# 64-point DFTs as three float32r products with operands split on ScalarE, VectorE and GpSimd, and steps placed by due date

## The chip, the cores and the metric

The kernel runs on one core of a Trainium2 chip. A core has five engines with a queue each, which run beside one another and wait for one another through semaphores: TensorE (PE; its weight loads are shown apart as PEld), VectorE (DVE), ScalarE (ACT), GpSimd (POOL) and SyncE (SP), which here only issues DMAs. The metric is the device time of one execution in microseconds (us), as the median of several runs.

## The reference

Two parts follow one another. The first is a circular convolution by FFT over the sequence: `X = rfft(x)` over 3008 positions for 8 batches and 256 channels, a product with a complex filter, and `irfft`. The second sends each of the 24064 tokens through a block with a rational activation:

```python
X = np.fft.rfft(x, axis=1);  Y = X * (filt_r + 1j * filt_i);  y = np.fft.irfft(Y, n=3008, axis=1)
h = y @ w_in                                    # 256 -> 2048
g = (a0 + a1*h + a2*h**2 + a3*h**3) / (1 + |b0|*|h| + |b1|*h**2 + 1e-6)
out = g @ w_out                                 # 2048 -> 256
```

Everything is float32, and the kernel must reach float32 accuracy.

## The kernel before

**Two number formats on TensorE.** A matmul whose operands are plain float32 is one instruction in the program and two records in the trace (x2). A float32r operand is one that was rounded when it was written; a matmul of float32r operands is one record. To keep the accuracy with float32r, an operand is split into `hi` (the rounded value) and `lo` (the rest, rounded), and a product is made of three matmuls: high weights by hi, high weights by lo, low weights by hi. The large products of the second part (h_u, lines 460 to 463, and o, lines 537 to 539) are made so. The convolution is in plain float32.

**The units.** The second part is cut into 47 token tiles of 512 and 16 slices of the hidden width: 752 units. A unit has six matmuls into a PSUM bank (h_u), a chain of ScalarE, GpSimd and VectorE operations that makes hi_u and lo_u, and six matmuls into o. The loop `pipeline` runs one step per unit, and step i issues on each engine what belongs to several units at once. The table ORDER gives the lags. On VectorE, in this order: hi_u of unit i-2 (line 514), then a convolution step if there is one, then `rest` of unit i-3 (line 522), `p` of unit i-1 (line 505), lo_u of unit i-3 (line 528). On GpSimd: the convolution step, then the product q_u by hi_u of unit i-2 (line 519), then line 500 for unit i-1. So `rest` of a unit waits for GpSimd's line 519, which was issued one step earlier. TensorE issues in step i: h_u of unit i, the convolution step, o of unit i-5 (i-6 for the first of a tile).

**The convolution.** Per batch the 3008 points are split as 47 by 64. Stage 1 has 16 matmuls s (line 300, 96 partitions); ScalarE copies each out of PSUM (s1e, line 263), and SP stores pairs of them in the DRAM scratch scr1 (line 304). Stage 2 loads it back (xin, line 339) and has, for 12 column blocks, the forward 64-point DFT y (line 348), VectorE's two products with the filter (lines 355 and 356), GpSimd's crosswise terms zw (four instructions, line 367) and their sum (line 372), and then the inverse 64-point DFT z (line 381), copied out of PSUM by ScalarE and VectorE in turn (lines 263 and 265) and stored in scr2. Stage 3 loads tl from scr2 and makes x (line 426), which ScalarE and VectorE split into the token operands xh and xl.

Batch one goes through all this before the loop. Batches two to eight (numbers 1 to 7 in the code) are spread over the steps of the loop by a generator `conv_items`, which yields before each s, y and z. The loop holds a credit that grows by RATES per step and pays COST for each such step; a batch may start EARLY units ahead. Stage 3 pieces come at steps 1 and 9 of a tile. GAP yields stand between stage 1 and stage 2. All engines but SP run in the order in which the program was written.

**Buffers.** Six PSUM banks are shared by the units and the convolution steps (class Banks: the bank free for longest is taken). zw has two buffers, `ev` two, xin four, filters f1 and f2 three each; z is made in place in f1.

## Time and profile before

| | |
|---|---|
| median of 3 runs | 2523.23 us (2522.63 to 2524.99) |
| the profiled execution | 2527.08 us |
| its span | 2525.1 us |
| busy share of the span | PE 98%, PEld 76%, DVE 90%, ACT 87%, POOL 74% |
| granted TensorE clock | 0.99 of full speed over the span |

The profile comes from one execution. A busy engine may be one whose instructions overlap: matmul records are modelled at their ends, so the pace of TensorE is read from starts. "Idle before" is time in which an engine stood still ahead of an instruction, and the releaser is what ended it. The timeline gives start, length, engine, line and operation of single instructions.

### The profile page before, as it was taken

Reading aid. Unit: us, or ns where it says so; the run is one execution under the profiler, and the core shown is the slowest. Engines: PE = TensorE matmul, PEld = TensorE weight load, DVE = VectorE, ACT = ScalarE, POOL = GpSimd, SP = SyncE. Lnnn points to the kernel's source line nnn. Section 1 sums busy time; section 2 is a strip of 40 time slices with the busy share of each in tenths; the row PEclk is TensorE's granted clock in tenths of the full one; section 3 lists DMA queues with packets and bytes.
Section 4 is the critical chain, followed back from the end, with each engine's and each line's share of the span. In section 5 each row is a group of like instructions: output and inputs, shape, how many; then the busy total and the mean of one; then the engine's idle time right before and its main releaser. Section 6 shows DMA issues by size and latency. Waiting matters only on the chain.

```text
span 2525.1 us, 35502 instructions
## 1 busy us (share of the span) xinstructions
PE 2464.8 (98%) x10456; PEld 1918.1 (76%) x10456; DVE 2264.6 (90%) x3573; ACT 2201.0 (87%) x4193; POOL 1856.3 (74%) x1984
## 2 busy tenths in 40 slices
PE   4799999999999999999999999999999999999998
PEld 1477777777777777878777777777777778888887
DVE  5789988999889998999889998899988999999998
ACT  4588889888988889888898889988898889999997
POOL 3468876887668876788668886688757887677776
PEclk8999999999999999999999999999999999999999
DMA  8643342222323222231322322222222211000000
GB/s 256 199 132 104 92 124 86 83 85 68 100 90 94 78 82 72 96 96 59 107 88 70 92 78 91 87 85 86 80 82 94 75 43 32 28 24 22 24 9 19
DMA packets 104364, 208.94 MB, mean 83 GB/s; under 512 B 9696, under 2 KB 59104, under 8 KB 104160
## 3 DMA queue, kind: packets, MB, share of 16 engines
q1 hardware_dynamic: 100944, 199.30, 25.8%
q10 hardware_dynamic: 3216, 7.27, 0.9%
q8 instruction: 85, 1.39, 0.2%
q14 instruction: 119, 0.97, 0.1%
HBM read 131.56 MB, written 74.97 MB: 82 GB/s over the span
## 4 chain that ended last, share of the span: by engine, by line
PE 89%; DVE 4%; POOL 2%; DMA 2%; issue 1%; ACT 1%; SPq 0%; ACTq 0%; DVEq 0%; POOLq 0%
PE o L538 13%; PE o L537 13%; PE o L539 13%; PE h_u L461 13%; PE h_u L460 13%; PE h_u L463 13%; PE x L426 4%; PE s L300 4%; PE y L348 3%; PE z L381 3%; DVE h_u L522 1%; POOL q_u L519 1%; POOL zw L367 1%; DMA scr<-s1e 1%; DVE h_u L505 1%
## 5 line engine op out<-in xcount | busy, mean ns | idle before, releaser
L519 POOL TENSOR_TENSOR q_u<-q_u,hi_u 128x512 f32<-128x512 f32 x752 | 975.1, 1297 | 470.6 <-DVE hi_u L514 451.8
L537 PE MATMUL o<-hi_u,wo_sb 128*128 128x512 f32 x1504 | 704.5, 468 | 0.0
L468 ACT ACTIVATE q_u<-h_u 128x512 f32<-128x512 f32 x752 | 450.3, 599 | 209.4 <-PE h_u L463 143.0
L522 DVE SCALAR_TENSOR_TENSOR h_u<-h_u,words_sb,q_u 128x512 f32<-128x512 f32 x752 | 564.0, 750 | 61.0 <-POOL q_u L519 59.6
L514 DVE SCALAR_TENSOR_TENSOR hi_u<-h_u,words_sb,a_u 128x512 fp32r<-128x512 f32 x752 | 557.4, 741 | 66.0 <-ACT a_u L490 64.1
L460 PE MATMUL h_u<-xh,wi_sb 128*128 128x512 f32 x1504 | 593.4, 395 | 1.8 <-DVE xl L438 1.2
L538 PE MATMUL o<-lo_u,wo_sb 128*128 128x512 f32 x1504 | 590.3, 393 | 2.8 <-DVE lo_u L528 2.8
L539 PE MATMUL o<-hi_u,wo_sb 128*128 128x512 f32 x1504 | 587.8, 391 | 0.0
L461 PE MATMUL h_u<-xl,wi_sb 128*128 128x512 f32 x1504 | 586.9, 390 | 0.2
L500 POOL TENSOR_SCALAR q_u<-q_u,words_sb 128x512 f32<-128x512 f32 x752 | 584.0, 777 | 1.3 <-ACT a_u L485 1.3
L505 DVE SCALAR_TENSOR_TENSOR h_u<-w_u,words_sb,h_u 128x512 f32<-128x512 f32 x752 | 559.9, 745 | 3.4 <-ACT w_u L475 3.4
L528 DVE TENSOR_TENSOR lo_u<-h_u,a_u 128x512 fp32r<-128x512 f32 x752 | 512.1, 681 | 0.1
L485 ACT ACTIVATE a_u<-q_u 128x512 f32<-128x512 f32 x752 | 475.6, 632 | 0.0
L490 ACT ACTIVATE a_u<-a_u 128x512 f32<-128x512 f32 x752 | 470.9, 626 | 0.0
L481 ACT ACTIVATE q_u<-q_u 128x512 f32<-128x512 f32 x752 | 469.3, 624 | 0.0
L463 PE MATMUL h_u<-xh,wi_sb 128*128 128x512 f32 x1504 | 463.9, 390 | 0.0
L475 ACT ACTIVATE w_u<-h_u 128x512 f32<-128x512 f32 x752 | 444.1, 590 | 0.3 <-POOL wi_sb L246 0.3
L538 PEld LDWEIGHTS o<-lo_u,wo_sb 128*128 128x128 f32 x1504 | 282.7, 188 | 113.1 <-issue 61.3
L537 PEld LDWEIGHTS o<-hi_u,wo_sb 128*128 128x128 f32 x1504 | 282.5, 188 | 112.8 <-issue 64.7
L460 PEld LDWEIGHTS h_u<-xh,wi_sb 128*128 128x128 f32 x1504 | 282.5, 188 | 70.1 <-DVE lo_u L528 5.8
L461 PEld LDWEIGHTS h_u<-xl,wi_sb 128*128 128x128 f32 x1504 | 282.6, 188 | 63.6 <-issue 3.1
L539 PEld LDWEIGHTS o<-hi_u,wo_sb 128*128 128x128 f32 x1504 | 282.4, 188 | 61.7
(95 smaller groups left out, 1874.4 us busy)
## 6 DMA issues: line engine op xcount, KB each, us to landing
xin<-xp SPq DMA_DIRECT2D x64, 384.0 KB, 3.8
scr<-s1e SPq DMA_DIRECT2D x64, 384.0 KB, 4.0
xin<-scr SPq DMA_DIRECT2D x48, 512.0 KB, 4.7
scr<-ev SPq DMA_DIRECT2D x96, 256.0 KB, 3.8
tl<-scr SPq DMA_DIRECT2D x64, 384.0 KB, 3.1
outT<-oe SPq DMA_DIRECT2D x47, 512.0 KB, 2.8
f<-fr SPq DMA_DIRECT2D x87, 256.0 KB, 4.1
f<-fi SPq DMA_DIRECT2D x87, 256.0 KB, 3.8
```

The costliest lines, as they stand in the source:

```text
L460: nc.tensor.matmul(o, w_in_part(0, f, cc), xh[:, cc, ts], start=cc == 0, stop=False)
L461: nc.tensor.matmul(o, w_in_part(0, f, cc), xl[:, cc, ts], start=False, stop=False)
L463: nc.tensor.matmul(o, w_in_part(1, f, cc), xh[:, cc, ts], start=False, stop=cc == 1)
L500: nc.gpsimd.tensor_scalar(out=self.q, in0=self.q, scalar1=AIK, scalar2=SGN, op0=ALU.mult, op1=ALU.add)
L505: v.scalar_tensor_tensor(out=H, in0=w, scalar=PK, in1=H, op0=ALU.add, op1=ALU.mult)
L514: nc.vector.scalar_tensor_tensor(out=self.hi, in0=self.H, scalar=self.p0, in1=self.a, op0=ALU.add, op1=ALU.mult)
L519: nc.gpsimd.tensor_tensor(out=self.q, in0=self.q, in1=self.hi.bitcast(F32), op=ALU.mult)
L522: nc.vector.scalar_tensor_tensor(out=self.H, in0=self.H, scalar=self.p0, in1=self.q, op0=ALU.add, op1=ALU.subtract)
L528: nc.vector.tensor_tensor(out=self.lo, in0=self.H, in1=self.a, op=ALU.mult)
L537: nc.tensor.matmul(o, w_out_part(0, f, dd), self.hi, start=f == 0, stop=False)
L538: nc.tensor.matmul(o, w_out_part(0, f, dd), self.lo, start=False, stop=False)
L539: nc.tensor.matmul(o, w_out_part(1, f, dd), self.hi, start=False, stop=f == 15)
```

## The change

The 64-point DFTs are made as three float32r matmuls in place of one float32 matmul: y in batches three to eight (72 of them), z in batches two to eight (84). The matrices are split once, at the end of the first batch (four small instructions). For y, the operand is split where stage 1 leaves PSUM: ScalarE writes hi (in place of its copy), and VectorE, at the end of the step, writes lo = PSUM - hi; scr1 then holds both halves, twice the bytes, with one store for each s and one load for each y. For z, ScalarE copies z to hi right after the inverse product before it, and GpSimd subtracts for lo, one step later, ahead of its other work of that step. The two halves lie in one buffer (tag raw). zw has one buffer in place of two.

The credit is gone. Each batch has a first step (`begin`) and a last one (`end`, three steps before its first stage 3 piece is wanted), and a convolution step is issued once the loop has reached its due place between them, in proportion to LOAD; TURN steps are kept free between stages 1 and 2.

```diff
+LOAD = dict(s=0.62, y=1.2, z=0.86), dict(s=0.76, y=1.03, z=0.86)
+REST = 3
...
+GAP = 1
+TURN = 4
...
-    scr1 = [dram.tile([K2, 128, C], F32, tag="scr1", name=f"scr1_{b}") for b in range(B)]
+    scr1 = [
+        dram.tile([K2, 128, 2, C], F32, tag="scr1", name=f"scr1_{b}") if b > 1
+        else dram.tile([K2, 128, C], F32, tag="scr1_0", name=f"scr1_{b}", bufs=2) for b in range(B)
+    ]
...
-            yield COST[0]
+            yield "s"
             k, pt = banks.tile(f"s1_{b}_{q}_{j}")
             nc.tensor.matmul(pt[:R1], a1_sb, xin[:, j], start=True, stop=True)
             yield
+            if b > 1:
+                split_rows(b, q, j, k, pt[:R1])
+                continue
             evac(EV1, ev[:, j], pt[:R1], 2 * q + j)
             banks.done(k, 0.5)
+        if b > 1:
+            return
...
+
+    def finish():
+        while pending:
+            pending.pop(0)()
+
+    def split_rows(b, q, j, bank, pt):
+
+        ev = conv.tile([R1, 2, 2, C], F32R, tag="ev", name=f"s1e{b}_{q}_{j}")
+        hi, lo = ev[:, :, 0], ev[:, :, 1]
+        pt = pt.rearrange("p (m c) -> p m c", c=C)
+        nc.scalar.activation(hi, pt, AF.Copy)
+
+        def lower():
+            v.tensor_tensor(out=lo, in0=pt, in1=hi.bitcast(F32), op=ALU.subtract)
+            banks.done(bank, 0.5)
+            m = 4 * q + 2 * j
+            dst = scr1[b].rearrange("k (g m) h c -> (k g) m (h c)", m=NH)[:, m : m + 2]
+            nc.sync.dma_start(dst.rearrange("r m c -> r (m c)"), ev.bitcast(F32).rearrange("p m h c -> p (m h c)"))
+
+        pending.append(lower)
+
...
+    def run_own(*key):
+        while own := [t for t in tasks if t[2] == key]:
+            tasks.remove(own[0])
+            own[0][3]()
...
+        def load_split(self, i):
+            if i < 12:
+                self.tin[i] = conv.tile([128, 2, 2, C], F32R, tag="xin", name=f"xin{self.b}_{i}", bufs=XB)
+                nc.sync.dma_start(
+                    self.tin[i].bitcast(F32), scr1[self.b][2 * i : 2 * i + 2].rearrange("k p h c -> p k h c")
+                )
+
+        def fetch(self, q):
+            (self.load_split if self.b > 1 else self.load)(q)
+
...
@@ -343,9 +398,16 @@
 
         def product(self, i):
             b, (q, j) = self.b, divmod(i, 2)
-            yield COST[1]
+            yield "y"
             bank, yt = banks.tile(f"y_{b}_{i}")
-            nc.tensor.matmul(yt, mats_sb[:, 0, :], self.flat(self.tin[q], j), start=True, stop=True)
+            if b > 1:
+                tin = self.tin.pop(i)
+                hi, lo = tin[:, :, 0], tin[:, :, 1]
+                nc.tensor.matmul(yt, fwd_sb[:, 0], hi, start=True, stop=False)
+                nc.tensor.matmul(yt, fwd_sb[:, 0], lo, start=False, stop=False)
+                nc.tensor.matmul(yt, fwd_sb[:, 1], hi, start=False, stop=True)
+            else:
+                nc.tensor.matmul(yt, mats_sb[:, 0, :], self.flat(self.tin[q], j), start=True, stop=True)
             yield
             self.z[i] = z, z2 = [self.flat(f_, j) for f_ in self.f[q]]
...
                 return
 
...
                 if WAITS[n]:
                     yield
             nc.gpsimd.tensor_tensor(out=z, in0=z, in1=zw, op=ALU.add)
+            if i == 0:
+                tasks.append((banks.now + 1, "post", (b, 0), lambda: self.split(0)))
+
+        def split(self, i):
+
+            if i == 12:
+                return
+            z = self.z[i][0]
+            part = conv.tile([128, 2, TT], F32R, tag="raw", name=f"zs{self.b}_{i}", bufs=1)
+            self.parts[i] = hi, lo = part[:, 0], part[:, 1]
+            nc.scalar.activation(hi, z, AF.Copy)
+
+            def lower():
+                nc.gpsimd.tensor_tensor(out=lo, in0=z, in1=hi.bitcast(F32), op=ALU.subtract)
+
+            tasks.append((banks.now + 1, "post", (self.b, i), lower))
 
         def inverse(self, i):
             b, (q, j) = self.b, divmod(i, 2)
             if j == 0:
                 self.ev[q] = self.tl("ev", q)
-            yield COST[2]
+            yield "z"
             bank, zt = banks.tile(f"z_{b}_{i}")
             z, z2 = self.z.pop(i)
-            nc.tensor.matmul(zt, mats_sb[:, 1, :], z, start=True, stop=b > 0)
-            if b == 0:
+            if b:
+                run_own(b, i)
+                hi, lo = self.parts.pop(i)
+                nc.tensor.matmul(zt, inv_sb[:, 0], hi, start=True, stop=False)
+                nc.tensor.matmul(zt, inv_sb[:, 0], lo, start=False, stop=False)
+                nc.tensor.matmul(zt, inv_sb[:, 1], hi, start=False, stop=True)
+            else:
+                nc.tensor.matmul(zt, mats_sb[:, 1, :], z, start=True, stop=False)
                 nc.tensor.matmul(zt, mats_sb[:, 2, :], z2, start=False, stop=True)
             yield
             evac(EV2 if b else "A", self.flat(self.ev[q], j), zt, i)
             banks.done(bank, 0.5)
+            if b:
+                self.split(i + 1)
...
         for i in range(13):
             if i < 12:
                 yield from s.product(i)
             if i > 0:
                 yield from s.inverse(i - 1)
+            if b > 1:
+                s.fetch(i + 2)
             if i % 2 == 0 and i // 2 + 2 < 6:
                 s.load_filter(i // 2 + 2)
-                s.load(i // 2 + 2)
...
         for _ in range(GAP):
             yield
+        finish()
         yield from stage2(b)
...
+        nc.scalar.activation(fwd_sb[:, 0], mats_sb[:, 0], AF.Copy)
+        nc.vector.tensor_tensor(out=fwd_sb[:, 1], in0=mats_sb[:, 0], in1=fwd_sb[:, 0].bitcast(F32), op=ALU.subtract)
+        nc.scalar.activation(inv_sb[:, 0], mats_sb[:, 1], AF.Copy)
+        nc.vector.tensor_tensor(out=inv_sb[:, 1], in0=mats_sb[:, 1], in1=inv_sb[:, 0].bitcast(F32), op=ALU.subtract)
...
+    latest = [g0 * G // T * 16 - 8 + XF for g0, _ in chunks]
+    for k in range(len(chunks) - 2, -1, -1):
+        latest[k] = min(latest[k], latest[k + 1] - 8)
+
+    def end(b):
+
+        return latest[8 * b] - REST
+
+    def begin(b):
+        return FIRST if b == 1 else end(b - 1)
+
+    def due(b, used, kind):
+        w = LOAD[b > 1]
+        total = 16 * w["s"] + 12 * (w["y"] + w["z"])
+        return begin(b) + (end(b) - begin(b) - TURN) * used / total + TURN * (kind != "s")
...
-            credit = min(credit + RATES[nxt > 1], 2.5)
...
-                if g1 * G <= t * T + RX and ((g0 if f > XF else g1) * G < T * (t + 2) or need < nxt):
+                if g1 * G <= t * T + RX and (i >= latest[xk] or need < nxt):
...
-            elif credit > 0 and i < n and not active and i >= last + PGAP and not (xgen and i > xi):
-                if gen is None and nxt < B and i >= FIRST and i >= 94 * nxt - 94 - EARLY:
-                    gen = conv_items(nxt)
-                    cost = next(gen)
-                if gen:
+            elif i < n and not active and i >= last + PGAP and not (xgen and i > xi):
+                if gen is None and nxt < B and i >= begin(nxt):
+                    gen, used = conv_items(nxt), 0
+                    kind = next(gen)
+                if gen and i >= due(nxt, used, kind):
                     next(gen)
-                    credit -= cost
+                    used += LOAD[nxt > 1][kind]
                     post.append("c")
...
             for name, lag in ORDER[:CPOS]:
                 step(lag, name)
+            run_tasks(i, "post")
...
+            run_tasks(i, "end")
+            finish()
```

**TensorE around y.** Batch five (number 4), block 4, step 295 before and step 316 after; h_u295 is the bank of unit 295, fwd_sb the split matrix, xin4_4 the loaded halves.

```order
L463 MATMUL h_u295_10782<-xh_613,wi_sb_76 128x512 x2
L348 MATMUL y_4_4_10789<-xin4_2_10311,mats_sb_78 128x512
L537 MATMUL o18_0_10751<-hi_u290_10690,wo_sb_77 128x512
L538 MATMUL o18_0_10751<-lo_u290_10738,wo_sb_77 128x512
L539 MATMUL o18_0_10751<-hi_u290_10690,wo_sb_77 128x512
```

After the change the same place reads:

```order
L552 MATMUL h_u316_11799<-xh_619,wi_sb_76 128x512 x2
L406 MATMUL y_4_4_11806<-xin4_4_11611,fwd_sb_79 128x512
L407 MATMUL y_4_4_11806<-xin4_4_11611,fwd_sb_79 128x512
L408 MATMUL y_4_4_11806<-xin4_4_11611,fwd_sb_79 128x512
L626 MATMUL o19_0_11587<-hi_u311_11715,wo_sb_77 128x512
L627 MATMUL o19_0_11587<-lo_u311_11765,wo_sb_77 128x512
L628 MATMUL o19_0_11587<-hi_u311_11715,wo_sb_77 128x512
```

One float32 matmul has become three float32r matmuls between the same neighbours; o follows five units behind h_u in both.

**GpSimd from one zw to the next.** The same batch, from the sum that belongs to block 4 to the zw of block 5; zs4_4 is the buffer of the split halves of block 4.

```order
L372 TENSOR_TENSOR f14_2_10305<-f14_2_10305,zw4_4_10806 128x512
L519 TENSOR_TENSOR q_u294_10769<-q_u294_10769,hi_u294_10833 128x512
L500 TENSOR_SCALAR q_u295_10801<-q_u295_10801,words_sb_81 128x512
L519 TENSOR_TENSOR q_u295_10801<-q_u295_10801,hi_u295_10865 128x512
L500 TENSOR_SCALAR q_u296_10837<-q_u296_10837,words_sb_81 128x512
L519 TENSOR_TENSOR q_u296_10837<-q_u296_10837,hi_u296_10905 128x512
L500 TENSOR_SCALAR q_u297_10869<-q_u297_10869,words_sb_81 128x512
L519 TENSOR_TENSOR q_u297_10869<-q_u297_10869,hi_u297_10934 128x512
L500 TENSOR_SCALAR q_u298_10909<-q_u298_10909,words_sb_81 128x512
L367 TENSOR_SCALAR zw4_5_10974<-f24_2_10306,sgn_sb_75 64x256 x4
L519 TENSOR_TENSOR q_u298_10909<-q_u298_10909,hi_u298_10965 128x512
```

After the change, from the same sum on:

```order
L434 TENSOR_TENSOR f14_2_11246<-f14_2_11246,zw4_4_11825 128x512
L608 TENSOR_TENSOR q_u315_11786<-q_u315_11786,hi_u315_11852 128x512
L589 TENSOR_SCALAR q_u316_11820<-q_u316_11820,words_sb_83 128x512
L608 TENSOR_TENSOR q_u316_11820<-q_u316_11820,hi_u316_11882 128x512
L589 TENSOR_SCALAR q_u317_11856<-q_u317_11856,words_sb_83 128x512
L608 TENSOR_TENSOR q_u317_11856<-q_u317_11856,hi_u317_11915 128x512
L589 TENSOR_SCALAR q_u318_11886<-q_u318_11886,words_sb_83 128x512
L448 TENSOR_TENSOR zs4_4_11923<-f14_2_11246,zs4_4_11923 128x512
L608 TENSOR_TENSOR q_u318_11886<-q_u318_11886,hi_u318_11957 128x512
L589 TENSOR_SCALAR q_u319_11919<-q_u319_11919,words_sb_83 128x512
L429 TENSOR_SCALAR zw4_5_12002<-f24_2_11247,sgn_sb_75 64x256 x4
L608 TENSOR_TENSOR q_u319_11919<-q_u319_11919,hi_u319_11993 128x512
```

The subtraction (line 448) stands between line 500 and line 519 of one step, so line 519 of that step comes behind it. zw of block 5 comes five steps after that of block 4 in both.

**VectorE at the end of a step with s.** Batch five, stage 1; s1e4 is the buffer of the split rows. Before, no VectorE instruction belongs to s, and a step there reads (units 251 to 253):

```order
L514 SCALAR_TENSOR_TENSOR hi_u252_9388<-h_u252_9307,words_sb_81,a_u252_9325 128x512
L522 SCALAR_TENSOR_TENSOR h_u251_9278<-h_u251_9278,words_sb_81,q_u251_9295 128x512
L505 SCALAR_TENSOR_TENSOR h_u253_9339<-w_u253_9359,words_sb_81,h_u253_9339 128x512
L528 TENSOR_TENSOR lo_u251_9400<-h_u251_9278,a_u251_9294 128x512
L514 SCALAR_TENSOR_TENSOR hi_u253_9419<-h_u253_9339,words_sb_81,a_u253_9357 128x512
```

After the change, in step 265, which holds the second s of the batch:

```order
L611 SCALAR_TENSOR_TENSOR h_u262_9902<-h_u262_9902,words_sb_83,q_u262_9933 128x512
L594 SCALAR_TENSOR_TENSOR h_u264_9978<-w_u264_9996,words_sb_83,h_u264_9978 128x512
L617 TENSOR_TENSOR lo_u262_10040<-h_u262_9902,a_u262_9932 128x512
L332 TENSOR_TENSOR s1e4_0_1_10031<-s1_4_0_1_10016,s1e4_0_1_10031 96x2x256
L603 SCALAR_TENSOR_TENSOR hi_u264_10063<-h_u264_9978,words_sb_83,a_u264_9994 128x512
```

The subtraction out of PSUM (line 332) stands behind lo_u and ahead of hi_u of the next step.

## Rows read from the trace of the kernel before

**Rows 1.** The page: the span, and busy time, share and instructions of each engine.

```profile
span 2525.1 us, 35502 instructions
...
PE 2464.8 (98%) x10456; PEld 1918.1 (76%) x10456; DVE 2264.6 (90%) x3573; ACT 2201.0 (87%) x4193; POOL 1856.3 (74%) x1984
```

**Rows 2.** Stretches in which the convolution is in stage 2 (206 to 324: batch two; the others: batches four, five and six): length, then busy us (and instructions) of PE, PEld, DVE, ACT and POOL, granted clock, DMA share, GB/s.

```profile
206.00:324.00 118.00, 117.50 (x493) 90.08 (x492) 109.82 (x172) 98.41 (x188) 102.58 (x120) 1.00 0.29 90
740.00:880.00 140.00, 140.00 (x598) 110.10 (x597) 132.00 (x209) 121.69 (x235) 119.25 (x136) 1.00 0.29 85
1030.00:1202.00 172.00, 171.88 (x745) 135.92 (x744) 162.10 (x255) 149.29 (x287) 142.70 (x161) 1.00 0.24 74
1320.00:1495.00 175.00, 174.62 (x755) 137.76 (x754) 162.93 (x256) 153.07 (x294) 141.94 (x161) 1.00 0.27 82
```

**Rows 3.** The timeline of TensorE in batch five, stage 2, from one y to the next: start us, length us. The rows of line 460 are the first matmul of a unit.

```profile
1082.79 0.39 PE L460 MATMUL h_u<-xh,wi_sb 128*128 128x512 f32 x1
...
1084.15 1.02 PE L348 MATMUL y<-xin,mats_sb 128*128 128x512 f32 x2
...
1086.40 0.39 PE L460 MATMUL h_u<-xh,wi_sb 128*128 128x512 f32 x1
...
1089.14 0.39 PE L460 MATMUL h_u<-xh,wi_sb 128*128 128x512 f32 x1
...
1090.50 1.02 PE L381 MATMUL z<-f,mats_sb 128*128 128x512 f32 x2
...
1091.59 0.40 PE L538 MATMUL o<-lo_u,wo_sb 128*128 128x512 f32 x1
...
1092.75 0.39 PE L460 MATMUL h_u<-xh,wi_sb 128*128 128x512 f32 x1
...
1095.48 0.39 PE L460 MATMUL h_u<-xh,wi_sb 128*128 128x512 f32 x1
...
1099.57 1.02 PE L348 MATMUL y<-xin,mats_sb 128*128 128x512 f32 x2
```

**Rows 4.** What VectorE waited for in the last three stretches of rows 2, in their order, the row of GpSimd's product from each: us in total, times, longest.

```profile
DVE h_u L522 <- POOL q_u L519: 7.9, 16, 1.0
...
DVE h_u L522 <- POOL q_u L519: 7.4, 17, 0.6
...
DVE h_u L522 <- POOL q_u L519: 7.5, 15, 0.8
```

**Rows 5.** The timeline of VectorE over the same y to y; in brackets, idle time before an instruction and what ended it.

```profile
1085.33 0.68 DVE L355 TENSOR_TENSOR f<-y,f 128x512 f32<-128x512 f32 x1
...
1087.84 0.68 DVE L528 TENSOR_TENSOR lo_u<-h_u,a_u 128x512 fp32r<-128x512 f32 x1
...
1089.55 0.76 DVE L522 SCALAR_TENSOR_TENSOR h_u<-h_u,words_sb,q_u 128x512 f32<-128x512 f32 x1 [0.37 <-POOL q_u L519]
...
1092.13 0.68 DVE L265 COPY ev<-z 128x512 f32<-128x512 f32 x1
...
1095.38 0.75 DVE L522 SCALAR_TENSOR_TENSOR h_u<-h_u,words_sb,q_u 128x512 f32<-128x512 f32 x1
...
1097.95 0.75 DVE L522 SCALAR_TENSOR_TENSOR h_u<-h_u,words_sb,q_u 128x512 f32<-128x512 f32 x1
...
1100.62 0.69 DVE L355 TENSOR_TENSOR f<-y,f 128x512 f32<-128x512 f32 x1
```

**Rows 6.** The timeline of GpSimd over the same stretch.

```profile
1086.17 1.96 POOL L367 TENSOR_SCALAR zw<-f,sgn_sb 64x256 f32<-64x256 f32 x4 [0.57 <-POOL q_u L500]
...
1094.88 0.78 POOL L500 TENSOR_SCALAR q_u<-q_u,words_sb 128x512 f32<-128x512 f32 x1
1095.75 1.30 POOL L519 TENSOR_TENSOR q_u<-q_u,hi_u 128x512 f32<-128x512 f32 x1
...
1098.19 1.30 POOL L519 TENSOR_TENSOR q_u<-q_u,hi_u 128x512 f32<-128x512 f32 x1 [0.37 <-DVE hi_u L514]
```

**Rows 7.** Groups by line over the whole span: count, then busy us, mean ns of one, idle us before them and what ended it.

```profile
L372 POOL TENSOR_TENSOR f<-f,zw 128x512 f32<-128x512 f32 x84 | 109.0, 1297 | 0.0
L348 PE MATMUL y<-xin,mats_sb 128*128 128x512 f32 x192 | 99.6, 602 | 19.5 <-issue 19.1 <-DVE ev L265 0.3
L381 PE MATMUL z<-f,mats_sb 128*128 128x512 f32 x180 | 92.4, 595 | 3.3 <-ACT fxl L329 3.3
L263 ACT ACTIVATE s1e<-s 96x512 f32<-96x512 f32 x128 | 75.1, 595 | 38.6 <-PE s L300 17.7 <-DMA scr<-s1e 12.4 <-DVE words_sb L187 7.8
...
L356 DVE TENSOR_TENSOR f<-y,f 128x512 f32<-128x512 f32 x90 | 61.1, 679 | 0.0
```

**Rows 8.** Two more stretches, columns as in rows 2: stage 1 of batch four falls into the first; in the second the loop has no stage 1 or 2 left to do.

```profile
614.00:722.00 108.00, 108.00 (x457) 82.88 (x457) 91.22 (x143) 97.98 (x189) 70.07 (x69) 1.00 0.27 83
2125.00:2400.00 275.00, 275.00 (x1252) 229.68 (x1251) 260.38 (x412) 263.90 (x509) 198.00 (x193) 1.00 0.07 22
```

**Rows 9.** The last stage 1 step of batch eight: SP's issues of the last store of scr1 and of the first load of it (timeline of SP).

```profile
1912.11 0.30 SPq L304 DMA_DIRECT2D scr<-s1e  x1
1915.14 0.38 SPq L339 DMA_DIRECT2D xin<-scr  x1
```

**Rows 10.** The page: DMA queue 1 (packets, MB, share of 16 engines), and loads of scr1 (count, KB each, median us from issue to landing).

```profile
q1 hardware_dynamic: 100944, 199.30, 25.8%
...
xin<-scr SPq DMA_DIRECT2D x48, 512.0 KB, 4.7
```

More of the change, by code (lines that the diff above doesn't have):

```diff
@@ L306, in stage1, with run_tasks @@
         )
+    pending = []
+    def finish():
[13 more added lines that the diff above has]
+        pending.append(lower)
+    tasks = []
+    def run_tasks(i, place):
+        ready = [t for t in tasks if t[0] < i or t[0] == i and t[1] == place]
+        for t in ready:
+            tasks.remove(t)
+            t[3]()
+    def run_own(*key):
+        while own := [t for t in tasks if t[2] == key]:
+            tasks.remove(own[0])
+            own[0][3]()
     class Stage2:
         def __init__(self, b):
-            self.b, self.f, self.tin, self.ev, self.z = b, {}, {}, {}, {}
+            self.b, self.f, self.tin, self.ev, self.z, self.parts = b, {}, {}, {}, {}, {}
         def tl(self, tag, q, **kw):
@@ L396, in stage2 @@
             s.load_filter(q)
-            s.load(q)
+            s.fetch(q)
         for i in range(13):
@@ L665, in pipeline @@
         sp = ExitStack()
-        gen, cost, credit, nxt = None, 0.0, 0.0, 1
+        gen, kind, used, nxt = None, None, 0, 1
         xgen, xk, xi = None, 2, 0
@@ L746, in pipeline @@
             elif active:
-                cost = next(gen, 0)
-                if cost is not None:
+                kind = next(gen, "")
+                if kind is not None:
                     active = None
-                if cost == 0:
+                if kind == "":
                     gen = None
```

12 lines of the change are left out of this document (6 added, 6 removed).

## Prediction

> **What bounds the kernel now.** I read the page first: TensorE is busy in 98% of the span, VectorE in 90%, ScalarE in 87%, GpSimd in 74% [rows 1]. These are averages, so the next view is the table by stretches. While the convolution is in stage 2, TensorE has no idle time worth a name (140.00 of 140 us, 171.88 of 172), VectorE is busy for 132.00 of 140 and 162.10 of 172, GpSimd for 119.25 of 140 [rows 2]. The reader is to see that three engines are nearly full there, not one.
>
> The timeline of TensorE gives its pace. From the first matmul of a unit to that of the next, a plain step takes 2.74 and 2.73 us; the step with y takes 3.61 and the step with z 3.61 [rows 3]. So a float32 product costs 3.61 - 2.735 = 0.875 us, and one of the twelve matmuls of a plain step 2.735 / 12 = 0.228.
>
> Then VectorE's waits. In three stage 2 stretches it waits for GpSimd's product 7.9, 7.4 and 7.5 us [rows 4]. Added to its busy time this leaves 140 - 132.00 - 7.9 = 0.1, 172 - 162.10 - 7.4 = 2.5 and 175 - 162.93 - 7.5 = 4.6 us: 7.2 of 487 us, or 1.5%. That is all the time in which the pair of VectorE and GpSimd is held up by anything but itself. Cycle by cycle it is the same: y to y is 1099.57 - 1084.15 = 15.42 us on TensorE [rows 3], and from the first filter product to the next 1100.62 - 1085.33 = 15.29 us on VectorE [rows 5]. TensorE sets the time, and the pair follows at 98 to 99% of it.
>
> There is a store between the two. The lo_u that VectorE writes in the step with y ends at 1087.84 + 0.68 = 1088.52 [rows 5]; TensorE reads it two steps later, behind z, at 1091.59 [rows 3], 3.1 us on. I count 2 us of it as usable, since the distance varies within a cycle.
>
> **The change part by part.**
>
> *The products.* 72 forward and 84 inverse DFTs, 156 in all, go from one float32 matmul to three float32r ones: from 0.875 to 3 x 0.228 = 0.684, a gain of 0.19 us each, 4.6 us for the 24 of a batch, 30 us for all. No row shows a float32r operand read in two pieces with a gap (hi and lo lie side by side). Bounds: it is as fast as the contiguous ones (0.228), or it takes twice as long, 1.37 a product, which is 0.49 more than before. I take the first, which is what every contiguous row shows, and keep the second as a rival.
>
> *Does the pair of VectorE and GpSimd let TensorE have it?* A batch's stage 2 lasts some 180 us. The pair can be faster there by its 1.5%, 2.7 us; TensorE can also use up the store of 2 us and get it back in stage 1. Against this stands GpSimd's new subtraction: 1297 ns by line 372, which is of the same shape [rows 7], 12 a batch, always ahead of the product that VectorE waits for. What a late product costs is in the cycle: line 519 at 1095.75 ends at 1097.05 [rows 6], and the VectorE instruction that needs it starts at 1097.95 [rows 5], so 0.90 us are spare, and 1.30 overrun them by 0.4. That is the case where z comes two steps after y. Where it comes three steps after, the delayed product is the one at 1098.19 [rows 6]; its reader comes behind both filter products of the next y (1100.62 + 1.2 = 1101.8), and 2.3 us are spare. In the new order z follows y by two steps in two or three of twelve cycles, elsewhere by three or four. I take 1.2 us a batch; bounds 0 and 12 x 0.98 = 12 (0.98 where VectorE does not have that cycle's copy of z, 0.6 us, either). So a batch of 4.6 possible gets 2.7 + 2.0 - 1.2 = 3.5, and six batches 21. The new order also does stage 2 in fewer steps (335 in place of 351 over six batches); each plain step had given the pair 2.735 - 2.57 (VectorE's step, 1095.38 to 1097.95 [rows 5]) = 0.16 us, so 2.5 go: 18.5.
>
> *Batch two* has only its inverse changed and its cycles are three to four steps long. GpSimd is busy for 102.58 of 118 us there [rows 2]; twelve subtractions add 15.6 and fill it. TensorE needs 118 - 12 x 0.19 = 115.7. So it ends between 2.3 us earlier and, if all of GpSimd's idle time is forced by its waits, 15.6 later. I take 3 later, nearer the first, since a late GpSimd finds its operands ready.
>
> *VectorE's subtractions of stage 1:* 96 at 680 ns (line 356 [rows 7]) are 65 us. In stage 1 VectorE is busy for 91.22 of 108 us [rows 8]; with 16 x 0.68 = 11 it is at 102. Hidden by TensorE; 65 if that cover were gone. A busier stage 1 leaves a slightly smaller store for stage 2, within the 2 us I took of 3.1.
>
> *ScalarE:* 84 new copies at 0.6 us (595 ns, line 263 [rows 7]), 50 us; in stage 2 it goes from 121.69 of 140 [rows 2] to about 126. Hidden. A copy of z must find GpSimd's sum done; that is two steps before at least.
>
> *DMAs:* 38 MB more on queue 1, which goes from 25.8% [rows 10] to about 31%, and 84 more issues of 0.3 to 0.4 us on SP [rows 9]. Hidden, except at the turn from stage 1 to 2. There the last store went out at 1912.11, the load behind it at 1915.14 [rows 9], and a load takes 4.7 us to land [rows 10]: 7.7 us after the copy. Now the subtraction comes in between, up to a step later, 7.7 + 3.4 = 11 us, with 1 us for s and its copy 12. In the new order y stands six or seven steps (over 16 us) behind the last s, but four (11 to 12 us) in batch seven. I take 1.5 us once; if all six turns were that short, 9.
>
> *The head:* four small instructions before the first stage 3 piece, 0.5 us.
>
> Sum: -18.5 + 3 + 1.5 + 0.5 = -13.5 us. The profiled execution took 2527.1, so 2513.6; it lay 3.9 above the median of the runs, 2523.2, on whose scale I forecast 2510.
>
> **The rivals.**
>
> *All of it.* TensorE stays the bound: 30 us, 2493. For it: TensorE hardly waits in any stretch of rows 2, and GpSimd's waits shrink when it is late. Against it: 15.29 of 15.42.
>
> *GpSimd's subtraction, from the step after each z.* If it delays VectorE in every cycle, not in two or three, the gain of a batch is 4.7 - 12 d for a delay d, gone at d = 0.39 us. The row shows 0.4 for the close case, 0.98 without the copy. At d = 0.5: 6 x 1.3 = 8, fewer steps 2.5, batch two 6, turns 2: about 18 slower, 2541. Against it: 2.3 us spare in the common spacing.
>
> *Nothing to see.* The pair keeps its 15.29 or so, the store is spent in the first cycles, batch two and the turns take back the rest: within 5 us of 2523.
>
> *VectorE sets the time throughout*, and TensorE's records only look full. Then 65 us more on it cost 2525 x 65 / 2265 = 72 us: 2595. Against it: VectorE has idle time in every stretch of rows 2, and TensorE's starts are evenly spaced. The Trainium skill speaks for it: "Perfetto Trace Analysis", section "Identifying the Most-Contended Engine", calls matmul busy time no good measure and goes by the busy share of weight loads. By that rule TensorE is at 76% [rows 1], VectorE at 90% is the engine to relieve, and the change loads the wrong one. The trace does not bear it out: where the loop has only units left, weight loads are busy for 229.68 of 275 us [rows 8], 84%, and TensorE still has no gap, so 84% is full here.
>
> *Operands in two pieces are slow:* 72 x 0.49 = 35 us slower, 2558.
>
> **How the numbers follow.** Forecast 0.45, all of it 0.17, nothing 0.17, GpSimd's delays 0.16, VectorE throughout 0.02, slow operands 0.03. The likeliest's own range is 2499 to 2519 (delays of 0 to 0.2 us a cycle, batch two from -2 to +8). The range for 8 in 10 reaches below to 2490, past "all of it", and above to 2531, into the delays. About 0.2%, 5 us, can be told from no change: faster 0.45 + 0.17 = 0.62, same 0.17, slower 0.21.
>
> **What would show it.** Right: in stage 2, steps with y or z 0.19 us shorter where TensorE does not wait; waits of TensorE for lo_u, absent now, towards the end of each stage 2, about 1 us a batch; VectorE without any wait there but for GpSimd; GpSimd busy 95% in stage 2 of batch two and TensorE waiting in it. Wrong: no waits of TensorE at all (all of it), or VectorE's waits for GpSimd at double their 7 to 8 us a stretch (the delays), or a product of three matmuls at over 0.7 us.

## The result, and the profile after

The changed kernel takes 2553.22 us (median of 5 runs, 2548.12 to 2554.50) against 2523.23 us for the kernel before (5 runs beside it, 2522.63 to 2525.06): a ratio of 1.0108 [1.0096, 1.0119], about 30 us slower. The forecast was 13 us faster, and the time lies outside its range. The profiled execution took 2548.51 us.

Three rows of the kernel before stand first. From its page, the chain that ended last, by engine:

```profile
PE 89%; DVE 4%; POOL 2%; DMA 2%; issue 1%; ACT 1%; SPq 0%; ACTq 0%; DVEq 0%; POOLq 0%
```

From its waits over the whole span, VectorE's for GpSimd's product and those of TensorE's weight loads for lo_u (us, times, longest):

```profile
DVE h_u L522 <- POOL q_u L519: 59.6, 125, 1.0
...
PEld h_u L460 <- DVE lo_u L528: 5.8, 13, 1.1
```

The page after: span, engines, chain.

```profile
span 2546.7 us, 36323 instructions
...
PE 2456.4 (96%) x10612; PEld 1945.3 (76%) x10612; DVE 2312.3 (91%) x3671; ACT 2246.2 (88%) x4279; POOL 1961.4 (77%) x2068
...
PE 63%; POOL 16%; DVE 9%; issue 5%; ACT 5%; DMA 2%; SPq 0%; POOLq 0%; ACTq 0%; DVEq 0%
```

Against [rows 1], TensorE is busy for 8 us less, and it idles 2546.7 - 2456.4 = 90.3 us where it idled 60.3. The span is 21.6 us longer: 30 us more of idle time and 8 us less of busy time, where the products were to take off 30. A kernel below with the same 10612 matmul records is busy for 2440.8 us, so some 16 us of the 2456.4 are no work of their own; what these may be is said in the last section. The chain says which engines the added time lies with: GpSimd's share went from 2% to 16%, VectorE's from 4% to 9%. The busy shares alone (POOL 74% to 77%) would not have told it.

Stage 2 of batches two, four, five and six after the change, columns as in [rows 2]:

```profile
200.00:327.00 127.00, 121.87 (x524) 95.55 (x523) 113.73 (x178) 108.56 (x207) 117.14 (x132) 1.00 0.30 84
830.00:960.00 130.00, 128.38 (x572) 104.62 (x572) 121.81 (x192) 117.74 (x225) 119.72 (x131) 1.00 0.33 94
1100.00:1285.00 185.00, 180.81 (x799) 147.51 (x798) 169.67 (x268) 165.35 (x316) 166.01 (x184) 0.99 0.31 90
1405.00:1600.00 195.00, 190.74 (x845) 156.18 (x844) 180.17 (x284) 174.88 (x334) 174.33 (x192) 0.99 0.32 96
```

TensorE, with at most 0.5 us of idle time in a stretch of [rows 2], now stands still for 5.1, 1.6, 4.2 and 4.3 us of these stretches; GpSimd went from 81 to 87% of such a stretch to 89 to 92%. The waits over the whole span say for what:

```profile
DVE h_u L611 <- POOL q_u L608: 88.8, 134, 1.9
...
PEld h_u L549 <- DVE lo_u L617: 47.8, 55, 2.6
...
PE h_u L549 <- DVE lo_u L617: 25.3, 33, 2.2
...
PEld z L463 <- POOL zs L448: 12.2, 5, 3.9
...
PE z L463 <- POOL zs L448: 10.0, 5, 3.4
...
PEld s L305 <- DVE s1e L332: 7.3, 21, 0.4
```

TensorE's matmuls wait 25.3 us for lo_u and 10.0 us for GpSimd's lower half of z. The first is a wait of **h_u**, not of o: lo_u is the last to read the PSUM bank of its unit, and a later h_u takes that bank. One such wait, at the first z of batch five, in the timeline (TensorE, VectorE and GpSimd mixed):

```profile
1115.34 1.30 POOL L448 TENSOR_TENSOR zs<-f,zs 128x512 fp32r<-128x512 f32 x1
...
1116.59 1.30 POOL L434 TENSOR_TENSOR f<-f,zw 128x512 f32<-128x512 f32 x1
...
1117.01 0.39 PE L462 MATMUL z<-zs,inv_sb 128*128 128x512 f32 x1
...
1117.69 0.39 PE L626 MATMUL o<-hi_u,wo_sb 128*128 128x512 f32 x1
...
1117.85 1.30 POOL L608 TENSOR_TENSOR q_u<-q_u,hi_u 128x512 f32<-128x512 f32 x1
...
1118.82 0.39 PE L628 MATMUL o<-hi_u,wo_sb 128*128 128x512 f32 x1
...
1119.18 0.76 DVE L611 SCALAR_TENSOR_TENSOR h_u<-h_u,words_sb,q_u 128x512 f32<-128x512 f32 x1 [1.86 <-POOL q_u L608]
...
1120.50 0.68 DVE L617 TENSOR_TENSOR lo_u<-h_u,a_u 128x512 fp32r<-128x512 f32 x1
...
1121.24 0.50 PE L549 MATMUL h_u<-xh,wi_sb 128*128 128x512 f32 x1 [2.03 <-DVE lo_u L617]
...
1125.46 0.39 PE L628 MATMUL o<-hi_u,wo_sb 128*128 128x512 f32 x1
```

The reader is to follow it downwards. On GpSimd the new subtraction (line 448) and the sum of the next block (line 434) stand one behind the other, 2.6 us, ahead of the product of line 608. VectorE waits 1.86 us for that product; its lo_u ends at 1120.50 + 0.68 = 1121.18, and h_u begins at 1121.24, after 2.03 us without work on TensorE. The DFT itself is as fast as reckoned: its three matmuls and no gap take 1117.69 - 1117.01 = 0.68 us. So does a y, whose operand is the one read in two pieces, 1144.35 - 1143.67 = 0.68 us, and 69 of the 72 y are below 0.7:

```profile
1143.67 0.39 PE L406 MATMUL y<-xin,fwd_sb 128*128 128x512 f32 x1
...
1144.35 0.39 PE L626 MATMUL o<-hi_u,wo_sb 128*128 128x512 f32 x1
```

The wait shown is of the rarest and longest kind. Counted over GpSimd's whole timeline, the sum stands directly behind the subtraction in 7 of 84 cases, once a batch, at its first z. In 27 cases it is zw of the next block, and in 50 the subtraction stands alone ahead of the product, as in the order shown ahead of the prediction. Of the 88.8 us that VectorE waits for GpSimd's product, 13.0 lie behind the 7, 22.0 behind the 27, and none behind the 50; the rest lies behind a zw or a sum without a subtraction, but for 1.0 us, and so did the 59.6 us before, but for 1.0. A case with zw and one alone, in the timeline of GpSimd, and VectorE's two instructions that read the products:

```profile
1145.62 1.30 POOL L448 TENSOR_TENSOR zs<-f,zs 128x512 fp32r<-128x512 f32 x1
1147.03 1.96 POOL L429 TENSOR_SCALAR zw<-f,sgn_sb 64x256 f32<-64x256 f32 x4
1149.07 1.30 POOL L608 TENSOR_TENSOR q_u<-q_u,hi_u 128x512 f32<-128x512 f32 x1
...
1158.61 1.31 POOL L448 TENSOR_TENSOR zs<-f,zs 128x512 fp32r<-128x512 f32 x1
1159.87 1.30 POOL L608 TENSOR_TENSOR q_u<-q_u,hi_u 128x512 f32<-128x512 f32 x1
```

```profile
1150.40 0.76 DVE L611 SCALAR_TENSOR_TENSOR h_u<-h_u,words_sb,q_u 128x512 f32<-128x512 f32 x1 [1.09 <-POOL q_u L608]
...
1162.59 0.75 DVE L611 SCALAR_TENSOR_TENSOR h_u<-h_u,words_sb,q_u 128x512 f32<-128x512 f32 x1
```

Groups by line over the span, columns as in [rows 7], for the two subtractions:

```profile
L448 POOL TENSOR_TENSOR zs<-f,zs 128x512 fp32r<-128x512 f32 x84 | 109.4, 1302 | 0.0
...
L332 DVE TENSOR_TENSOR s1e<-s,s1e 96x512 fp32r<-96x512 f32 x96 | 65.2, 679 | 5.7 <-ACT s1e L329 5.7
```

### The profile page after: what moved, and what is told of

Same layout as the page of the kernel before. It is cut to its first block, busy times and chain, and to the rows that moved or that the text cites. A ratio compares the mean times of both kernels' runs of the same rounds, so it can differ in the third digit from the quotient of the medians.

```text
span 2546.7 us, 36323 instructions
## 1 busy us (share of the span) xinstructions
PE 2456.4 (96%) x10612; PEld 1945.3 (76%) x10612; DVE 2312.3 (91%) x3671; ACT 2246.2 (88%) x4279; POOL 1961.4 (77%) x2068
## 4 chain that ended last, share of the span: by engine, by line
PE 63%; POOL 16%; DVE 9%; issue 5%; ACT 5%; DMA 2%; SPq 0%; POOLq 0%; ACTq 0%; DVEq 0%
PE h_u L549 9%; PE h_u L550 9%; PE h_u L552 9%; PE o L627 9%; PE o L626 9%; PE o L628 9%; POOL q_u L608 5%; PE s L305 4%; POOL zw L429 4%; PE x L515 3%; POOL q_u L589 3%; POOL f L434 3%; DVE h_u L611 2%; DVE h_u L594 2%; DVE hi_u L603 2%
## 5 line engine op out<-in xcount | busy, mean ns | idle before, releaser
L611 DVE SCALAR_TENSOR_TENSOR h_u<-h_u,words_sb,q_u 128x512 f32<-128x512 f32 x752 | 564.2, 750 | 89.5 <-POOL q_u L608 88.8
L626 PE MATMUL o<-hi_u,wo_sb 128*128 128x512 f32 x1504 | 644.5, 429 | 0.0
L549 PE MATMUL h_u<-xh,wi_sb 128*128 128x512 f32 x1504 | 598.0, 398 | 28.4 <-DVE lo_u L617 25.3
L628 PE MATMUL o<-hi_u,wo_sb 128*128 128x512 f32 x1504 | 586.0, 390 | 0.0
L549 PEld LDWEIGHTS h_u<-xh,wi_sb 128*128 128x128 f32 x1504 | 282.7, 188 | 112.0 <-DVE lo_u L617 47.8
L552 PEld LDWEIGHTS h_u<-xh,wi_sb 128*128 128x128 f32 x1504 | 283.5, 188 | 59.9
```

What stands on the lines that cost most here:

```text
L549: nc.tensor.matmul(o, w_in_part(0, f, cc), xh[:, cc, ts], start=cc == 0, stop=False)
L552: nc.tensor.matmul(o, w_in_part(1, f, cc), xh[:, cc, ts], start=False, stop=cc == 1)
L611: nc.vector.scalar_tensor_tensor(out=self.H, in0=self.H, scalar=self.p0, in1=self.q, op0=ALU.add, op1=ALU.subtract)
L626: nc.tensor.matmul(o, w_out_part(0, f, dd), self.hi, start=f == 0, stop=False)
L628: nc.tensor.matmul(o, w_out_part(1, f, dd), self.hi, start=False, stop=f == 15)
```

## The experiments

The theory after the result: VectorE and GpSimd have nothing to give, a late lo_u stops h_u through its PSUM bank, and GpSimd's subtraction makes it late. Rivals: the due dates are to blame, or the forward part's work on VectorE, or the first z of a batch, which waits for its lower half.

**The parts alone.** Three kernels: the due dates with every DFT in float32; the forward part with the inverse undone; the inverse part with the forward undone. The two undoings, each at its core:

```diff
-            if b > 1:
+            if False:
                 tin = self.tin.pop(i)
```

```diff
-            if b:
-                run_own(b, i)
-                hi, lo = self.parts.pop(i)
...
+            nc.tensor.matmul(zt, mats_sb[:, 1, :], z, start=True, stop=b > 0)
```

> Due dates alone: all 64-point DFTs stay in float32, no operand is split. Theory S (GpSimd's subtraction for z makes VectorE late, and TensorE's h_u, which takes the PSUM bank that lo_u of five units before gives back, waits for it): as before, 2523 within 6 us. Theory D (the new places of the steps cost by themselves: y of blocks 0 and 1 two steps apart, z of block 0 soon behind): 2540 or more. Theory V (VectorE's subtraction in stage 1 is what costs): as before, 2523.

Measured: 2525.33 us, ratio 1.0003 [0.9993, 1.0013]. The due dates cost nothing.

> Forward DFTs in float32r, inverse in float32: VectorE's subtraction in stage 1 is there, GpSimd's for z is not. Theory S: 72 x 0.19 = 14 us gained on a1, less a few us of waits for banks, 2509 to 2516. Theory D: a1's loss less 14, some 2530. Theory V: slower than a1, 2535 or more.

Measured: 2521.12 us, 0.9986 [0.9977, 0.9996]: 3 us of the 14 that 72 x 0.19 would give. TensorE waits where it had not, in this kernel's waits:

```profile
PEld h_u L539 <- DVE lo_u L607: 19.6, 38, 1.1
```

> Inverse DFTs in float32r, forward in float32: GpSimd's subtraction is there, VectorE's in stage 1 is not. Theory S: 84 x 0.19 = 16 us gained and 45 us of waits for banks and for the split of the first z: 2545 to 2555. Theory D: a1's loss less 16. Theory V: 2507 to 2512.

Measured: 2543.75 us, 1.0070 [1.0053, 1.0087]. The inverse is the harmful part: 18 us slower by itself, by its ratio. By the ratios the two parts add up to 14 us, the whole change to 27: together they cost some 13 us more than apart.

**The split without its use.** The inverse's halves are made, and one float32 matmul reads z as before; the forward part is undone.

```diff
+            if b:
+                run_own(b, i)
+                self.parts.pop(i)
+            nc.tensor.matmul(zt, mats_sb[:, 1, :], z, start=True, stop=b > 0)
```

> Due dates alone with the split of z added and not used: ScalarE's copies and GpSimd's subtractions are there, all 64-point DFTs stay in float32, so TensorE saves nothing. If TensorE's saving of 16 us on the inverse DFTs reached the end in the run with the inverse alone (2544), this one takes 2556 to 2564. If the saving never arrived, since VectorE and GpSimd set the time of stage 2, it takes 2541 to 2547, the same as with the products in float32r.

Measured: 2543.22 us, 1.0075 [1.0057, 1.0093], the same within the intervals as the inverse with its faster matmuls. Of the 84 x 0.19 = 16 us that TensorE saves there, nothing to be told from noise reaches the end; the making of the halves alone costs as much as the whole inverse part. One thing differs besides: here z does not wait for its lower half, and with the inverse alone TensorE waits 9.0 us for it, so a part of the 16 may go there. VectorE's row is almost that of the changed kernel:

```profile
DVE h_u L597 <- POOL q_u L594: 85.6, 130, 1.9
...
PEld h_u L535 <- DVE lo_u L603: 24.7, 29, 1.9
```

**Without the subtraction.** All of the change, but the lower half of z is neither made nor used; the second matmul reads the upper half again, so TensorE has as much to do.

```diff
             def lower():
-                nc.gpsimd.tensor_tensor(out=lo, in0=z, in1=hi.bitcast(F32), op=ALU.subtract)
+                pass
...
-                nc.tensor.matmul(zt, inv_sb[:, 0], lo, start=False, stop=False)
+                nc.tensor.matmul(zt, inv_sb[:, 0], hi, start=False, stop=False)
```

> All of the change without GpSimd's subtraction: the second of the three inverse matmuls reads the upper half again, so TensorE, ScalarE and VectorE have the same work, and the lower half of z is left out of the result. Theory S: GpSimd's load was the cost; 2500 to 2512, VectorE's wait for GpSimd at 60 to 67 us. Rival: ScalarE's copy, which waits for GpSimd's sum (16 us in the changed kernel), holds ScalarE's queue: 2530 or more.

Measured: 2517.36 us, 0.9971 [0.9960, 0.9982]. By the ratios this is 1.4% below the changed kernel's ratio, 35 us, so a subtraction costs 35 / 84 = 0.42 us on average. ScalarE's 84 copies are still in this kernel, so they are not the cause. Without it the change gains 7 us, less than either end of what I expected. VectorE waits for GpSimd about as before the change (59.6 us there), and TensorE still waits for lo_u:

```profile
DVE h_u L611 <- POOL q_u L608: 64.8, 132, 1.0
...
PEld h_u L549 <- DVE lo_u L617: 33.2, 52, 1.2
```

**Other places for the subtraction.** On VectorE in place of GpSimd; at the end of the step, behind GpSimd's other work; and with the first z of each batch two steps later.

```diff
-                nc.gpsimd.tensor_tensor(out=lo, in0=z, in1=hi.bitcast(F32), op=ALU.subtract)
+                nc.vector.tensor_tensor(out=lo, in0=z, in1=hi.bitcast(F32), op=ALU.subtract)
```

> All of the change, but the lower half of z is subtracted by VectorE in place of GpSimd, at the same place. Theory S: GpSimd's waits go back to those of before; VectorE has 84 x 0.6 = 50 us more on an engine that TensorE already waits for: 2525 to 2545, with VectorE's wait for GpSimd at 60 us and TensorE still waiting for lo_u. Theories D and V: as the changed kernel, 2545 to 2555.

Measured: 2567.69 us, 1.0169 [1.0152, 1.0186]: worse than the change itself, against my expectation. VectorE's waits for GpSimd fall back (59.3 us in 127 waits), but its own 59 us more delay lo_u all the more:

```profile
PEld h_u L549 <- DVE lo_u L617: 73.8, 95, 1.3
```

So neither of the pair has the time for this subtraction at that place.

```diff
-            tasks.append((banks.now + 1, "post", (self.b, i), lower))
+            tasks.append((banks.now + 1, "end", (self.b, i), lower))
```

> All of the change, but GpSimd's subtraction stands at the end of its step, behind the product that VectorE waits for, in place of ahead of it. Theory P (the place ahead of the product makes VectorE late): VectorE's wait for GpSimd falls from 89 us to 60 to 70, and the time to 2530 to 2540. Theory L (GpSimd's load counts, whatever the place): VectorE's wait stays at 80 to 95 us and the time at 2548 to 2556.

Measured: 2612.38 us, 1.0344 [1.0325, 1.0362], a miss for both theories: VectorE's wait for GpSimd did not fall but rose, to 109.1 us. The lower half is then not ready when z is due, and TensorE waits for it itself:

```profile
PEld z L463 <- POOL zs L448: 63.1, 24, 5.8
```

```diff
+            if i == 1 and b > 0:
+                yield
+                yield
             if i > 0:
                 yield from s.inverse(i - 1)
```

> All of the change, and the first z of a batch is held back by some three steps more. Theory S1 (11 us of the loss are TensorE waiting at the first z for GpSimd's subtraction, because the two first y stand two steps apart and GpSimd is late there): 2538 to 2546, and no wait of z for zs. Theory S2 (GpSimd's load over the whole stage counts, not the place): 2550, the same as the changed kernel.

Measured: 2544.28 us, 1.0080 [1.0062, 1.0098]. z's weight loads wait 5.1 us in place of 12.2, and the kernel is some 7 us faster than the change: the first z's wait for its lower half is a part of the loss, not its core. What GpSimd does there is untouched by this run: the sum still stands directly behind the subtraction 7 times, and VectorE's wait for GpSimd is 87.6 us.

**Relieving VectorE.** The copies of z out of PSUM go to ScalarE alone (42 fewer on VectorE, 0.68 us each), in the forward part alone, in the whole change, and in the kernel before as a control.

```diff
-EV1, EV2, EVO = "A", "AV", "AV"
+EV1, EV2, EVO = "A", "A", "AV"
```

> Forward DFTs alone in float32r, and every copy of z out of PSUM on ScalarE, so VectorE has 42 copies of 0.6 us (25 us) less in stage 2. Theory pair (VectorE with its waits for GpSimd already filled stage 2 before the change, and TensorE's saving is lost in waits for lo_u): 3 to 11 us faster than the run with the forward DFTs alone (2521), 2510 to 2518. Theory other (those waits come from single events, the stage's start or the turn): 2519 to 2523, unchanged.

Measured: 2514.34 us, 0.9962 [0.9948, 0.9976]: 10 of the 14 us arrive.

> All of the change, and every copy of z on ScalarE. Theory pair: VectorE's load and GpSimd's waits add up, so 25 us less on VectorE give 5 to 15 us: 2537 to 2548. Theory GpSimd alone (GpSimd sets the time of stage 2, VectorE only follows it): within 4 us of the changed kernel, 2549 to 2555.

Measured: 2539.11 us, 1.0053 [1.0036, 1.0070]: 14 us better than the change, still slower than before.

> The kernel before with every copy of z on ScalarE, a control: TensorE set its time, with 6 us of waits for lo_u at h_u, so relieving VectorE gives at most those: 2518 to 2526. If it gains 10 us or more, the kernel before was not bound by TensorE.

Measured: 2522.63 us, 0.9995 [0.9985, 1.0005]. The same relief is worth nothing in the kernel before. There TensorE sets the time, as the prediction read it; VectorE becomes a limit as soon as TensorE is made faster.

**The banks.** The kernel before with five PSUM banks in place of six, to see whether the banks tie TensorE to VectorE.

```diff
-    banks = Banks(8 - T * 2 // TT)
+    banks = Banks(7 - T * 2 // TT)
```

> The kernel before with five PSUM banks for units and convolution steps in place of six, so that h_u takes over the bank of a lo_u one unit younger whenever a step holds one. It measures how much of the distance between VectorE and TensorE could be given up. If the 3.1 us from lo_u to o were free to use, as the prediction had it, a step less costs little: 2523 to 2535. If h_u's wait for the bank is what counts and it had 0.3 to 0.6 us to spare: 2600 or more, with TensorE waiting for lo_u at most h_u.

Measured: 2755.54 us, 1.0916 [1.0898, 1.0935]. One bank is worth 231 us, so the distance through the banks is short indeed. But the waits are not mostly those of h_u, as I had expected; the convolution's matmuls wait longer (z for its operand, GpSimd's sum, and x for a bank):

```profile
PEld x L426 <- DVE lo_u L528: 61.9, 86, 1.6
...
PEld z L381 <- POOL f L372: 46.4, 33, 2.1
...
PEld h_u L460 <- DVE lo_u L528: 18.9, 26, 3.3
```

**Relieving GpSimd too.** Besides the copies, half of the zw instructions (168 of 336) go from GpSimd to ScalarE.

```diff
+                    if k:
+                        nc.scalar.activation(zw[o_, cs], z2[n_, cs], AF.Copy, scale=sg[n_])
+                    else:
+                        nc.gpsimd.tensor_scalar(
...
```

> Forward DFTs alone in float32r, copies of z and half of zw on ScalarE: GpSimd's chain at each y is 1 us shorter, so VectorE's wait for it falls below 50 us. If VectorE with these waits still bounds stage 2 (12 us of waits for lo_u are left in the run without this): 2508 to 2513. If ScalarE becomes late: 2518 or more.

Measured: 2509.45 us, 0.9939 [0.9923, 0.9956]: 15 us, as much as the 72 products save on TensorE. Moving zw was not tried in the kernel before; there TensorE's matmuls wait 3.9 us for lo_u in all, so little could come of it.

> The run without GpSimd's subtraction (the lower half of z is left out of the result), with the copies of z and half of zw on ScalarE: VectorE and GpSimd both relieved. If the saving of TensorE, 30 us, is real and only the pair kept it back: 2494 to 2503. If some of it was never there (operands in two pieces, three weight loads): 2508 or more, with TensorE not waiting for lo_u.

Measured: 2500.82 us, 0.9900 [0.9883, 0.9916]: 24 of 30 us arrive.

> All of the change, every copy of z on ScalarE, and two of the four instructions of zw on ScalarE, which takes 2 x 0.48 = 0.96 us of GpSimd's 1.3 us for the subtraction off again, 81 us in all. If GpSimd's time is what the subtraction costs, most of the 26 us between the run without the subtraction and the changed kernel... comes back: 2510 to 2525. If ScalarE then holds things up (it gets 168 instructions of some 0.4 us, 67 us), 2530 or more, with waits for ScalarE in VectorE's and GpSimd's rows.

Measured: 2504.18 us, 0.9915 [0.9899, 0.9932]. With the whole change in it, this kernel is faster than the changed kernel and than the one before. The subtraction costs 3 us here, where it cost 35. Its engines, its chain, and its waits:

```profile
PE 2440.8 (98%) x10612; PEld 1945.9 (78%) x10612; DVE 2286.8 (91%) x3629; ACT 2311.3 (92%) x4489; POOL 1879.5 (75%) x1900
...
PE 76%; ACT 10%; DVE 7%; issue 3%; POOL 2%; DMA 1%; SPq 0%; ACTq 0%; POOLq 0%; DVEq 0%
```

```profile
DVE h_u L614 <- POOL q_u L611: 25.6, 46, 1.6
...
PEld h_u L552 <- DVE lo_u L620: 6.5, 12, 0.9
```

GpSimd's share of the chain is back at the 2% of before, VectorE's wait for it is 25.6 us in place of 88.8, and TensorE's for lo_u 6.5 in place of 47.8. ScalarE now stands second in the chain.

## Why the prediction was wrong

To see where each term fell, one profiled execution of each kernel is cut at the starts of the first and the last matmul that belong to stage 2 of a batch, by the timeline of TensorE. With the due dates all of these kernels issue the same units in each part: 43 in stage 2 of batch two, 335 in that of the six other batches, 232 between the stages 2. "Relieved" means that the copies of z and half of zw are on ScalarE. Times in us:

| kernel | stage 2, batch two | stage 2, six others | between |
|---|---|---|---|
| due dates alone | 144.2 | 1080.8 | 759.4 |
| forward part | 144.3 | 1073.0 | 762.8 |
| inverse part | 153.3 | 1092.1 | 758.8 |
| the change without the subtraction | 143.2 | 1070.6 | 762.8 |
| the change | 153.2 | 1092.1 | 762.5 |
| the change, both relieved | 144.3 | 1056.7 | 762.2 |
| no subtraction, both relieved | 141.3 | 1056.6 | 762.0 |

*The products: right.* 0.68 us each, and 30 us less on TensorE to be had; the kernel with both of the pair relieved and no subtraction shows 24 of them, and 27 in its stages 2; between these it loses 2.6 again. Operands in two pieces are not slow, and that rival falls.

*The step that failed first: the store, and the pair's 1.5%.* The prediction let a batch take 2.7 us from the pair's lag and 2 us from "a store" of 3.1 us, read from lo_u's end at 1088.52 to the o that reads it at 1091.59. But lo_u has a second effect: it frees a PSUM bank, and what takes the bank comes sooner than o. Followed through class Banks, in the order of the steps, this bank goes to the z at 1090.50, 1.98 us behind lo_u. The lo_u one unit before and the one behind it give theirs to the h_u at 1086.40 and 1092.75 [rows 3]; these lo_u are, in VectorE's timeline before:

```profile
1084.07 0.68 DVE L528 TENSOR_TENSOR lo_u<-h_u,a_u 128x512 fp32r<-128x512 f32 x1
...
1090.87 0.68 DVE L528 TENSOR_TENSOR lo_u<-h_u,a_u 128x512 fp32r<-128x512 f32 x1
```

So 1086.40 - 1084.75 = 1.65 and 1092.75 - 1091.55 = 1.20 us lie between, less than the 2 us that were counted as usable. And the 1.5% was not time to spare: "held up by nothing but itself" is what an engine looks like that is about to be the bound. The rival "nothing to see" named it, and that is how the forward part by itself came out. The change without the subtraction tests the step: it was to end the six batches 6 x 4.7 = 28.2 us earlier, and their stages 2 are 1080.8 - 1070.6 = 10.2 us shorter, 1.7 a batch. Which of the two, store or lag, fell short by how much was not separated. In the whole kernel the steps without the subtraction give -28 + 2 = -26 us (pair and store 28.2, fewer steps 2.5, batch two 2.3 us earlier; head and turn 2); measured were -7.

*The step that was mis-sized: GpSimd's subtraction.* Taken at 1.2 us a batch and, with batch two, at 12 to 13 us in all; measured 35. In stage 2 of the six batches it was to cost 7.2 and cost 1092.1 - 1070.6 = 21.5 us. The 0.90 us of spare time in [rows 5, 6] was set against one instruction of 1.30, in two or three of twelve cycles. Where the subtraction stood alone, VectorE waited in none of the 50 cases. The cost arose where zw or the sum stood with it ahead of the product, in 34 of 84, five of twelve cycles, with 0.8 and 1.9 us of wait on average. The rival "GpSimd's subtraction" had the delay, its break-even at 0.39 us per cycle, and 2541 us; the measured 0.42 lies above that point, and its sign was right, but it let the delay fall in every cycle. It fell short of 2553 since it, too, gave the pair what the kernel without the subtraction shows it did not have. I gave it 0.16.

The two steps fall short by 26 - 7 = 19 and 35 - 12.5 = 22.5 us; together that is the miss, 43 us by the medians and 41 by the ratio.

*Batch two* was taken at 3 us later, and its stage 2 takes 9.0 us longer than with the due dates alone; without the subtraction it is 1.0 shorter, so the subtraction was taken at 5.3 us there and cost 10.0. With both of the pair relieved it costs 3.0 there and 0.1 in the six others. TensorE idles 5.1 us of 127 there, 0.5 of 118 before [rows 2], and GpSimd is at 92%, near the 95% named. *Stage 1's subtractions* on VectorE were to be hidden. Between the stages 2 the change takes 3.1 us more than the due dates alone, every kernel of the table with the forward part 762.0 to 762.8 us, and the inverse part none more: they cost some half a microsecond a batch, whether VectorE is relieved in stage 2 or not. *The turns and the head:* no y waits for a DMA, and the due dates cost nothing; what was put down for turns and head, 2 us, was no error that matters.

The table's terms, -10.2 for the six batches, 21.5 for the subtraction in them, 9.0 for batch two and 3.1 between, give 23.4 us; the two profiled executions, the change and the due dates alone, differ by 2546.7 - 2522.5 = 24.2.

*VectorE throughout:* the forward part loads VectorE with 2312.7 us, 48 more than before, and is not slower; and relieving VectorE before the change gains nothing. The rule of the Trainium skill that was weighed there ("Perfetto Trace Analysis", section "Identifying the Most-Contended Engine"), taken by its busy share of weight loads alone, would have named VectorE for relief before the change, and the control does not bear it out; after the change the relief does pay. The section names a second measure beside it, the share of peak FLOP/s, which was not worked out here.

*What stays open:* why the two parts cost more together than their sum. The table shows where: alone, the forward part makes stage 2 of the six batches 7.8 us shorter; beside the inverse part it makes it no shorter at all, 1092.1 in both.

## What to carry to other kernels

When one engine is at 100% and two others at 94% and 85%, a saving on the first is worth only what the second round allows: before pricing it, measure the distance from each producer to every reader, and to whoever waits for the buffer that it frees, and take the shortest. Work that makes an operand cheaper for the full engine has to be paid where there is room. Here ScalarE had it, with 1% of the chain before, though its busy share (87%) was above GpSimd's (74%). The same change was 1.1% slower with its cost on GpSimd alone and 0.85% faster with other work moved off the pair. The price of one more instruction is not the same everywhere: count the cases by what stands beside it, since here 50 of 84 cost VectorE no wait. A control that relieves the suspected engine in the old kernel tells in one run whether it was the bound.
